# Output-projection weights loaded in runs of two rows: what follows for the head dimension, and for a kernel that waits for its loads

## The chip, the cores and the metric

The kernel runs on one core of a Trainium2 chip. The metric is the device time of one execution in microseconds (us). "Span" is the time from the first to the last instruction in the records of that execution; it is about 1.8 us shorter than the time.

## The reference, cut to what matters

```python
# B = 8 sequences, one new token each; 32 heads of 128; 4096 cached keys and values; D = 640
xn = layernorm(x)
q  = (xn @ wq)                                   # 8 x 32 heads x 128
p  = softmax(q . k_cache * 128**-0.5)            # per sequence and head, over 4096 keys
o  = p . v_cache                                 # 8 x 32 x 128
out = x + o.reshape(8, 32 * 128) @ wo + mlp(layernorm(xn))      # wo: 4096 x 640
```

Everything is bf16. The two caches are 537 MB together (64 loads of 4 MB each); `wo` is 5.2 MB. So this is a kernel that streams memory.

## The kernel before

The work is cut into 64 tiles: `t = hg * 8 + b`, head group `hg` of 4 heads (`HT = 4`), sequence `b`. For a tile, K and V are one 4 MB load each, with 32 KB contiguous per partition. Two buffers for K, two for V. The output weights of a head group (512 rows of 640) are loaded once per 8 tiles; row `a * 128 + d` of a group goes to partition `d`, slot `a`:

```python
for hg in range(NG - 1):
    ld(hg * B + 3.65, wo_sb[:, :, :],
       lambda hg=hg: A_wo[span(hg, HT * P), :].rearrange("(a p) n -> p a n", p=P), ["wo"], "wo")
wo_last = A_wo[(H - HT) * P:H * P, :].rearrange("(a p) n -> p a n", p=P)
ld(T - 0.1, wo_sb[:, 0:HT - 1, :], wo_last[:, 0:HT - 1, :], ["wo"], "wo")     # the last group: 3 + 1 heads
ld(T - 0.09, wo_sb[:, HT - 1, :], wo_last[:, HT - 1, :], ["wo3"], "wo3")
```

The value matmuls (L621 in the profile) take V as the moving operand, four 32-key blocks of 512 columns in four column groups of the array (these matmuls overlap: 16 of them in the tail last 380 ns each by their records and 1.04 us together):

```python
r = e.matmul(PV_ps[32 * ct:32 * ct + HT * 4, t % 2, :],
             P_sb[:, i, m, :, :].rearrange("p a c -> p (a c)"),
             vv[:, 4 * m:4 * m + 4, :].rearrange("p a d -> p (a d)"),      # vv: V as p, key, d
             start=(q == 0), stop=(q == wide - 1))
```

ACT copies the result to `E_sb` (L640); small matmuls pick the right rows and turn it over (`pe_ex`, L646; in the last tile also L653), so that the head dimension lies on the partitions; then, once per two tiles, DVE divides by the row sums (L665):

```python
add("dve", np_, lambda e: e.tensor_tensor(
    dst, OT_ps.rearrange("p (a g) -> p a g", a=HT),                        # dst: oTn_sb, or oL_sb in the last group
    rinv_sb[:, g % 2, :].rearrange("p (a g) -> p a g", a=HT), ALU.mult), ...)
```

The projection multiplies slot by slot (L688 in the loop, L675 at the end). The end of the program is a chain: last quarter of the last V tile lands, 32 short value matmuls (L631), ACT copy, one small matmul, the division, eight projection matmuls, the copy to `out_sb`, the store.

Of the kernel before, what the change touches and what calls it, by code (L numbers as in the profile page):

```python
# [5 lines left out]
ALU = alu_op_type.AluOpType  # L6
# [5 lines left out]
P = 128  # L12
# [3 lines left out]
class _Op:  # L16
    __slots__ = ("pos", "seq", "eng", "fn", "R", "W", "X", "sem", "idx", "clock", "waits", "sig", "ticket", "seq2")


class _Sched:  # L20
# [12 lines left out]

    def add(self, eng, pos, fn, R=(), W=(), X=(), sem=None, sig=False):
        o = _Op()
        o.pos, o.seq, o.eng, o.fn, o.R, o.W, o.X, o.sem = pos, len(self.ops), eng, fn, R, W, X, sem
        o.sig = sig
        self.ops.append(o)
# [165 lines left out]
def bass_parallel_sum__gqa_block_cached__mixer_channel_mlp__decode_kernel(  # L204
# [13 lines left out]
    B, _, D = A_x.shape  # L218
    _, H, SK, DH = A_k_cache.shape
    F = B_w1.shape[1]  # L220
    HT = 4
# [3 lines left out]
    T = NG * B  # L225
    GT = 2
# [9 lines left out]
    FR = F - FC * P  # L236
    SCALE = float(DH) ** -0.5
    NK, NV, NS = 2, 2, 4
    SR = 2
    assert DH == P and D % P == 0 and H % HT == 0 and B == 8 and NJ == 128  # L240

# [3 lines left out]
    with ExitStack() as es:  # L245
# [4 lines left out]
        KV_sb = sb("KV_sb", [P, NK + NV, NJ * P], BF)  # L250
        KT_sb = sb("KT_sb", [P, NS, BK, P], BF)
        wo_sb = sb("wo_sb", [P, HT, D], BF)
# [23 lines left out]
        Y2_sb = sb("Y2_sb", [P, ND // 2, P // 2], BF)  # L276
        S_sb = sb("S_sb", [P, SR, GT, NJ], F32)
        P_sb = sb("P_sb", [P, GT, NJ // 4, HT, 4], BF)
# [7 lines left out]
        rinv_sb = sb("rinv_sb", [P, 2, HT * GT], F32)  # L286
        oTn_sb = sb("oTn_sb", [P, HT, B], BF)
        oL_sb = sb("oL_sb", [P, HT, B], BF)
# [7 lines left out]
        C2_ps = ps("C2_ps", [P, 512], F32)  # L296
        ACC_ps = ps("ACC_ps", [P, 512], F32)
        TRF = TR_ps[:, :, :].bitcast(F32)
        M1T_ps = CH_ps[0:GT, 0:P]
        NB_ps = CH_ps[:, P:P + GT]  # L300
        OT_ps = C2_ps[:, 0:HT * GT]
# [16 lines left out]
        add = sch.add  # L318
# [4 lines left out]

        def vview(t):
            return KV_sb[:, NK + t % NV, :].rearrange("p (j d) -> p j d", d=P)

        def span(i, n):

            return slice(i * n, (i + 1) * n) if isinstance(sch.turn, int) else bass.ds((sch.turn + i) * n, n)
# [22 lines left out]
        def dve_const2(e):  # L352
# [9 lines left out]
            W=["identneg", "onesb", "sel", "oTn", "wo"] + [(s, i) for s in ("Pt", "rs") for i in range(GT)])  # L362


        def ld(pos, dst, src, W, sem, R=()):
            add("sp", pos, lambda e: e.dma_start(dst, src() if callable(src) else src), R=R, W=W, sem=sem)  # L366
# [16 lines left out]
        for t in range(T):  # L383
# [5 lines left out]
            R = (["wqfree"], ["wqfree", "w1free", "hfree"])[t] if t < NV else []  # L389
# [3 lines left out]
        ld(-95.2, w1_sb, B_w1.rearrange("(k c) f -> k c f", c=DC), ["w1"], "w1")  # L393
        ld(-95.1, w2_sb[:, 0:FC, :], B_w2[0:FC * P, :].rearrange("(k c) n -> k c n", c=FC), ["w2"], "w2")
        ld(-95.0, w2_sb[0:FR, FC, :], B_w2[FC * P:F, :], ["w2r"], "w2r")
        for hg in range(NG - 1):
            ld(hg * B + 3.65, wo_sb[:, :, :],
               lambda hg=hg: A_wo[span(hg, HT * P), :].rearrange("(a p) n -> p a n", p=P), ["wo"],
               "wo")

        wo_last = A_wo[(H - HT) * P:H * P, :].rearrange("(a p) n -> p a n", p=P)
        ld(T - 0.1, wo_sb[:, 0:HT - 1, :], wo_last[:, 0:HT - 1, :], ["wo"], "wo")
        ld(T - 0.09, wo_sb[:, HT - 1, :], wo_last[:, HT - 1, :], ["wo3"], "wo3")


        def layernorm(n, pos, src, src_res, dst, dst_res):
# [21 lines left out]
        def transposed(w, pos, src, src_res):  # L428
# [16 lines left out]
            R=["x", "b2"], W=["xb2"])  # L445
# [60 lines left out]
        def scores(t):  # L506
# [27 lines left out]
            def act_s(e):  # L534
                for a in range(HT):
                    s = slice(a * PG, (a + 1) * PG)
                    r = e.activation(S_sb[s, g % SR, i, 0:JP],  # L537
                                     S_ps[s, 0:JP * HT].rearrange("p (j a) -> p j a", a=HT)[:, :, a], ACT.Copy)
                return r
            add("act", t - 0.04, act_s, R=["S"], W=[("SP", g % SR, i)], X=["S"])  # L540

# [67 lines left out]
        def values(t):  # L609
            hg, b = t // B, t % B  # L610
            g, i = t // GT, t % GT
            vv = vview(t)
            p0 = pvpos(t)
            last = t == T - 1
            NQ = NJ // 16
            wide = NQ - 2 if last else NQ
            for q in range(NQ):
                def pe_pv(e, q=q):
                    for ct in range(4):
                        m = 4 * q + ct  # L620
                        r = e.matmul(PV_ps[32 * ct:32 * ct + HT * 4, t % 2, :],  # L621
                                     P_sb[:, i, m, :, :].rearrange("p a c -> p (a c)"),
                                     vv[:, 4 * m:4 * m + 4, :].rearrange("p a d -> p (a d)"),
                                     start=(q == 0), stop=(q == wide - 1))
                    return r

                def pe_pv_last(e, q=q):
                    for ct in range(4):
                        m = 4 * q + ct
                        for c in range(4):  # L630
                            r = e.matmul(PV_ps[32 * ct:32 * ct + HT, 1 - t % 2, 0:P], P_sb[:, i, m, :, c],  # L631
                                         vv[:, 4 * m + c, :], start=(q == wide and c == 0),
                                         stop=(q == NQ - 1 and c == 3))
                    return r
                k = t % 2 if q < wide else 1 - t % 2
                add("pe", p0 + 0.02 * q + 0.1 * (q >= wide), pe_pv if q < wide else pe_pv_last,
                    R=[("V", t % NV, q), ("Pt", i)], W=[("PV", k)], X=[("PVb", k)])

            def evac(pos, k, n):
                add("act", pos, lambda e: e.activation(E_sb[:, k, 0:n], PV_ps[:, k, 0:n], ACT.Copy),  # L640
                    R=[("PV", k)] + ["wo"] * (t % GT and not last), W=[("E", k)], X=[("PVb", k)])
            OT_i = OT_ps.rearrange("p (a g) -> p a g", a=HT)[:, :, i]

            def pe_ex(e):
                for c in range(4):
                    r = e.matmul(OT_i, E_sb[:, t % 2, c * P:(c + 1) * P], sel_bf[:, c:HT * 4:4],  # L646
                                 start=(c == 0), stop=(c == 3 and not last))
                return r
            evac(p0 + (0.13 if last else 0.22), t % 2, 4 * P)
            add("pe", p0 + (0.14 if last else 0.28), pe_ex, R=[("E", t % 2), "sel"], W=["OT"], X=["C2"])  # L650
            if last:
                evac(p0 + 0.27, 1 - t % 2, P)
                add("pe", p0 + 0.28, lambda e: e.matmul(OT_i, E_sb[:, 1 - t % 2, 0:P], sel2_bf[:, :], start=False,  # L653
                                                       stop=True), R=[("E", 1 - t % 2), "sel"], W=["OT"], X=["C2"])

        def finish(g):
            hg, b0 = g // GPH, (g % GPH) * GT
            np_ = pvpos(g * GT + GT - 1) + 0.38

            tail = g >= NGRP - GPH  # L660
            res = "oL" if tail else "oTn"
            dst = (oL_sb if tail else oTn_sb)[:, :, b0:b0 + GT]
            if g <= NGRP - GPH + 1:
                add("dve", np_ - 0.004, lambda e: e.memset(oTn_sb[:, :, :], 0.0), W=["oTn", "oTn0"])  # L664
            add("dve", np_, lambda e: e.tensor_tensor(  # L665
                dst, OT_ps.rearrange("p (a g) -> p a g", a=HT),
                rinv_sb[:, g % 2, :].rearrange("p (a g) -> p a g", a=HT), ALU.mult),
                R=["OT", ("rinv", g % 2), "oTn0"], W=[res], X=["C2"])

        w = D // 2  # L670

        def pe_last(e, heads):
            for a in heads:
                for k in range(2):
                    r = e.matmul(TRF[32 * k:32 * k + B, 0, 0:w], oL_sb[:, a, :], wo_sb[:, a, k * w:(k + 1) * w],  # L675
                                 start=False, stop=(a == HT - 1), skip_group_check=True)
            return r
        LAST = pvpos(T - 1) + 0.4
        add("pe", LAST, lambda e: pe_last(e, range(HT - 1)), R=["wo", "oL", "base_ps"], X=[("TR", 0)])
        add("pe", LAST + 0.01, lambda e: pe_last(e, [HT - 1]), R=["wo3"], W=["fin"], X=[("TR", 0)])  # L680

        def project(g):

# [16 lines left out]
        def pe_zero(e):  # L700
            for n in range(2):
# [4 lines left out]
                                          start=True, stop=False, skip_group_check=True),  # L706
            R=["zeros"], W=["ACC"], X=["ACC"])
# [14 lines left out]
        def pe_hidden(e):  # L722
# [10 lines left out]
            R=[it_h], W=["h"], X=[it_h])  # L733

        def pe_hidden_t(e):
# [7 lines left out]
            R=[it_t], W=["hT"], X=[it_t])  # L743

        def pe_mlp2(e):
# [11 lines left out]
            R=["mlp", "xb2"], W=["xb2"], X=[("PVb", 0), ("PVb", 1)])  # L757
# [6 lines left out]
            R=["ACC"], W=["resT"], X=["ACC"])  # L764
# [21 lines left out]
        for pos, n in ((pvpos(T - 2) + 0.25, 2), (pvpos(T - 1) + 0.075, 4), (pvpos(T - 1) + 0.115, 3), (pvpos(T - 1) + 0.2, 1)):  # L786
# [3 lines left out]
            R=["fin"], W=["out0"], X=[("TR", 0)])  # L790
        add("act", END + 2, lambda e: e.activation(out_sb[:, w:D], TRF[32:32 + B, 0, 0:w], ACT.Copy),
            R=["fin"], W=["out1"], X=[("TR", 0, "act")])
# [51 lines left out]
```

## Time and profile before

| | |
|---|---|
| time, median of 3 | 1290.62 us |
| span of the profiled run | 1288.9 us |
| moved by DMA | 552 MB, 428 GB/s |
| busy: DVE, PE, ACT | 87%, 50%, 39% |

From the page of the kernel before: the head line and the busy shares of its engines, three rows in 40 slices of the span (digits are tenths; PEclk is the granted clock of the tensor engine), the count of DMA packets by size, the chain of waits by engine, and the DMA queue that loads instructions.

```profile
span 1288.9 us, 19855 instructions
...
PE 644.0 (50%) x7931; PEld 408.5 (32%) x7934; DVE 1121.8 (87%) x584; ACT 497.2 (39%) x1243; POOL 0.2 (0%) x4
...
PEclk9955555555655555555555555656556555555557
DMA  9999999999999999999999999999999999999998
...
DMA packets 23536, 552.00 MB, mean 428 GB/s; under 512 B 2313, under 2 KB 6497, under 8 KB 6498
...
q8 instruction: 8, 0.13, 0.0%
...
DMA 80%; DVE 9%; PE 8%; issue 3%; ACT 0%; SPq 0%; DVEq 0%
```

The DMA row is full from end to end: the loads are the bound. DVE at 87% looks close, but it is slack: it waits for K, 74.9 us in all. Of the 6497 packets under 2 KB, 2313 are tiny and 4184 have 1280 bytes; 4096 of these are rows of `wo`.

From the timeline of the kernel before, the DMA issues of the sync engine around one weight load and at the next (columns: start, duration of the issue, queue, line, operation, destination and source):

```profile
410.32 0.38 SPq L366 DMA_DIRECT2D wo_sb<-in_A_wo_dram  x1
422.45 0.33 SPq L366 DMA_DIRECT2D KV_sb<-in_A_k_cache_dram  x1
...
441.81 0.33 SPq L366 DMA_DIRECT2D KV_sb<-in_A_k_cache_dram  x1
...
463.07 0.33 SPq L366 DMA_DIRECT2D KV_sb<-in_A_k_cache_dram  x1
...
567.55 0.38 SPq L366 DMA_DIRECT2D wo_sb<-in_A_wo_dram  x1
```

A weight load is queued at 410.32 and the next one, a head group later, at 567.55: 157.23 us for 8 tiles and one weight load. Usually K loads are issued 19.4 us apart (422.45 to 441.81; 19.43 on average); in the gap in which the weights go through the queue it is 21.3 us (441.81 to 463.07). That is the price of one weight load: 1.83 us against the average.

From the timeline of the kernel before, the end of the program (columns: start, duration, engine, line, operation, out<-in with shapes, count, and in brackets the idle time before it with its releaser):

```profile
1284.25 0.65 PE L631 MATMUL PV_ps<-KV_sb,P_sb 128*4 128x128 bf16 x32 [0.70 <-DMA KV_sb<-in_A_v_cache_dram]
1285.00 0.28 ACT L640 ACTIVATE E_sb<-PV_ps 128x128 bf16<-128x128 f32 x1 [1.99 <-PE PV_ps L631]
...
1285.33 0.18 PE L653 MATMUL C_ps<-sel_bf,E_sb 128*128 128x4 bf16 x1 [0.42 <-ACT E_sb L640]
1285.55 0.17 DVE L665 TENSOR_TENSOR oL_sb<-C_ps,rinv_sb 128x8 bf16<-128x8 f32 x1 [6.17 <-PE C_ps L653]
...
1285.77 0.71 PE L675 MATMUL TR_ps<-wo_sb,oL_sb 128*8 128x320 bf16 x8 [0.26 <-DVE oL_sb L665]
...
1286.52 0.48 DVE L789 CAST out_sb<-TR_ps 8x320 bf16<-8x320 f32 x1 [0.81 <-PE TR_ps L675]
```

Here every step waits for the one before: from the division's start (1285.55) to the projection's (1285.77) it is 0.22 us, and anything added here is added to the time.

### The profile page before, as it was taken

Reading aid. Unit: us, or ns where it says so; the run is one execution under the profiler, and the core shown is the slowest. Engines: PE = TensorE matmul, PEld = TensorE weight load, DVE = VectorE, ACT = ScalarE, POOL = GpSimd, SP = SyncE. Lnnn points to the kernel's source line nnn. Section 1 sums busy time; section 2 is a strip of 40 time slices with the busy share of each in tenths; the row PEclk is TensorE's granted clock in tenths of the full one; section 3 lists DMA queues with packets and bytes.
Section 4 is the critical chain, followed back from the end, with each engine's and each line's share of the span. In section 5 each row is a group of like instructions: output and inputs, shape, how many; then the busy total and the mean of one; then the engine's idle time right before and its main releaser. Section 6 shows DMA issues by size and latency. Waiting matters only on the chain.

```text
span 1288.9 us, 19855 instructions
## 1 busy us (share of the span) xinstructions
PE 644.0 (50%) x7931; PEld 408.5 (32%) x7934; DVE 1121.8 (87%) x584; ACT 497.2 (39%) x1243; POOL 0.2 (0%) x4
## 2 busy tenths in 40 slices
PE   2654455454454455454445444444544554455456
PEld 1433233233333233233233232232332332333332
DVE  4989999898898898898988988988889888889885
ACT  1444344334344234343243442443432443423432
POOL 0000000000000000000000000000000000000000
PEclk9955555555655555555555555656556555555557
DMA  9999999999999999999999999999999999999998
GB/s 408 424 426 427 435 427 438 427 428 434 429 433 431 429 431 432 430 433 429 428 436 428 434 427 430 432 432 432 427 431 431 434 429 429 434 429 432 431 431 358
DMA packets 23536, 552.00 MB, mean 428 GB/s; under 512 B 2313, under 2 KB 6497, under 8 KB 6498
## 3 DMA queue, kind: packets, MB, share of 16 engines
q1 hardware_dynamic: 23488, 551.80, 99.9%
q8 instruction: 8, 0.13, 0.0%
q14 instruction: 6, 0.05, 0.0%
q10 hardware_dynamic: 34, 0.02, 0.0%
HBM read 551.80 MB, written 0.01 MB: 428 GB/s over the span
## 4 chain that ended last, share of the span: by engine, by line
DMA 80%; DVE 9%; PE 8%; issue 3%; ACT 0%; SPq 0%; DVEq 0%
DMA KV_sb<-in_A_v_cache_dram 76%; PE PV_ps L621 7%; DVE Y_sb L549 5%; DMA KV_sb<-in_A_k_cache_dram 2%; DVE Y_sb L553 2%; DMA KV_sb<-in_A_wq_dram 2%; DVE S_sb L556 2%; DVE M_sb L568 0%; SPq L366 0%; PE CH_ps L570 0%; PE TR_ps L675 0%; PE PV_ps L631 0%; PE TR_ps L461 0%; DVE rinv_sb L602 0%; DVEq L178 0%
## 5 line engine op out<-in xcount | busy, mean ns | idle before, releaser
L549 DVE TENSOR_TENSOR Y_sb<-KV_sb,qbc_sb 128x6144 bf16<-128x6144 bf16 x128 | 429.1, 3353 | 89.3 <-DMA KV_sb<-in_A_k_cache_dram 74.9
L556 DVE TENSOR_REDUCE S_sb<-Y_sb 128x48 f32<-128x3072 bf16 x128 | 429.2, 3353 | 4.4
L520 ACT ACTIVATE KT_sb<-TR_ps 128x1024 bf16<-128x1024 bf16 x256 | 254.6, 1020 | 228.5 <-PE TR_ps L517 227.0
L621 PE MATMUL PV_ps<-KV_sb,P_sb 128*16 128x512 bf16 x2040 | 225.0, 620 | 139.9 <-DMA KV_sb<-in_A_v_cache_dram 139.7
L517 PE MATMUL TR_ps<-ident_bf,KV_sb 128*128 128x128 bf16 x2048 | 250.2, 310 | 73.7 <-DMA KV_sb<-in_A_k_cache_dram 73.7
L553 DVE TENSOR_TENSOR Y_sb<-Y_sb 128x3072 bf16<-128x3072 bf16 x128 | 225.0, 1758 | 4.4
L517 PEld LDWEIGHTS TR_ps<-ident_bf,KV_sb 128*128 128x128 bf16 x2048 | 202.0, 142 | 84.3 <-DMA KV_sb<-in_A_k_cache_dram 78.3
L527 PE MATMUL S_ps<-qk_sb,KT_sb 128*128 128x4 bf16 x2048 | 98.2, 170 | 136.2 <-ACT KT_sb L520 134.3
L640 ACT ACTIVATE E_sb<-PV_ps 128x512 bf16<-128x512 f32 (+1 forms) x65 | 38.5, 593 | 319.1 <-PE PV_ps L621 317.1
L621 PEld LDWEIGHTS PV_ps<-KV_sb,P_sb 128*16 128x16 bf16 x2040 | 63.3, 124 | 251.8 <-DMA KV_sb<-in_A_v_cache_dram 145.2
L527 PEld LDWEIGHTS S_ps<-qk_sb,KT_sb 128*128 128x128 bf16 x2048 | 86.4, 109 | 167.4 <-ACT KT_sb L520 167.4
L588 ACT ACTIVATE P_sb<-S_sb,NB_sb 32x128 bf16<-32x128 f32 x256 | 101.9, 398 | 3.8
L646 PE MATMUL C_ps<-sel_bf,E_sb 128*128 128x4 bf16 x256 | 17.0, 172 | 135.1 <-DVE rinv_sb L602 113.2
L582 ACT ACTIVATE NB_sb<-CH_ps 128x2 f32<-128x2 f32 (+1 forms) x33 | 5.7, 172 | 171.4 <-PE CH_ps L578 171.4
L570 PE MATMUL CH_ps<-ident_f,M_sb 128*2 128x128 f32 (+1 forms) x33 | 12.1, 366 | 116.3 <-DVE M_sb L568 116.3
L646 PEld LDWEIGHTS C_ps<-sel_bf,E_sb 128*128 128x128 bf16 x256 | 11.5, 104 | 165.0 <-DVE rinv_sb L602 112.6
L537 ACT ACTIVATE S_sb<-S_ps 32x32 f32<-32x32 f32 x256 | 48.3, 189 | 32.2 <-PE S_ps L527 29.9
L588 ACT ACTIVATION_READ_ACCUMULATOR P_sb<-S_sb,NB_sb 32x1 f32 x256 | 47.0, 184 | 0.0
L570 PEld LDWEIGHTS CH_ps<-ident_f,M_sb 128*2 128x2 f32 (+1 forms) x33 | 2.7, 80 | 119.2 <-DVE M_sb L568 119.2
L664 DVE MEMSET oTn_sb<- 128x16 uint32 x30 | 2.2, 72 | 31.1 <-PE ACC_ps L688 31.1
L572 DVE TENSOR_REDUCE M_sb<-CH_ps 2x4 f32<-2x128 f32 (+1 forms) x33 | 9.2, 279 | 15.1 <-PE CH_ps L570 15.1
L599 PEld LDWEIGHTS C_ps<-rs_sb,ones_f 128*128 128x128 f32 x64 | 14.0, 274 | 25.4 <-issue 22.0
(96 smaller groups left out, 201.9 us busy)
## 6 DMA issues: line engine op xcount, KB each, us to landing
KV_sb<-in_A_k_cache_dram SPq DMA_DIRECT2D x64, 4096.0 KB, 26.8
KV_sb<-in_A_v_cache_dram SPq DMA_DIRECT2D x63, 4096.0 KB, 35.2
KV_sb<-in_A_wq_dram SPq DMA_DIRECT2D x1, 5120.0 KB, 23.8
wo_sb<-in_A_wo_dram SPq DMA_DIRECT2D x7, 640.0 KB, 30.9
KV_sb<-in_B_w_dram SPq DMA_DIRECT2D x1, 2160.0 KB, 39.1
w_sb<-in_B_w_dram SPq DMA_DIRECT2D x1, 2080.0 KB, 44.1
KV_sb<-in_A_v_cache_dram SPq DMA_DIRECT2D x1, 2048.0 KB, 12.6
KV_sb<-in_A_v_cache_dram SPq DMA_DIRECT2D x2, 1024.0 KB, 15.2
```

The source lines that it names most:

```text
L517: r = e.transpose(TR_ps[:, it.box[0], jj * P:(jj + 1) * P], kv[:, n * BK + jj, :], ident_bf[:, :])
L520: add("act", t - 0.59 + 0.12 * n, lambda e: e.activation(KT_sb[:, m % NS, :, :].rearrange("p a b -> p (a b)"), TR_ps[:, it.box[0], :], ACT ...
L527: r = e.matmul(S_ps[:, c:c + HT], KT_sb[:, m % NS, jj, :], qk_sb[:, :, i], start=True, stop=True)
L537: r = e.activation(S_sb[s, g % SR, i, 0:JP], S_ps[s, 0:JP * HT].rearrange("p (j a) -> p j a", a=HT)[:, :, a], ACT.Copy)
L549: return e.tensor_tensor(y, kv[:, j0:j1, :], qbc_sb[:, g % 2, i, :][:, None, :].to_broadcast([P, nj, P]), ALU.mult)
L553: lambda e, y=y, y2=y2: e.tensor_tensor(y2, y[:, :, 0:P // 2], y[:, :, P // 2:P], ALU.add),
L556: lambda e, y2=y2, j0=j0, j1=j1: e.tensor_reduce(S_sb[:, g % SR, i, j0:j1], y2, AX.X, ALU.add),
L570: add("pe", c - 0.715, lambda e: e.transpose(M1T_ps[0:n, :], M1_sb[:, 0:n], ident_f[:, :]), R=["M1", "identf"], W=["M1T"], X=["CH"])
L588: r = e.activation(P_sb[s, i, :, a, :], S_sb[s, g % SR, i, :].rearrange("p (m c) -> p m c", c=4), ACT.Exp, bias=NB_sb[s, g % 2, i:i + 1], ...
L621: r = e.matmul(PV_ps[32 * ct:32 * ct + HT * 4, t % 2, :], P_sb[:, i, m, :, :].rearrange("p a c -> p (a c)"), vv[:, 4 * m:4 * m + 4, :].rea ...
L640: add("act", pos, lambda e: e.activation(E_sb[:, k, 0:n], PV_ps[:, k, 0:n], ACT.Copy), R=[("PV", k)] + ["wo"] * (t % GT and not last), W=[ ...
L646: r = e.matmul(OT_i, E_sb[:, t % 2, c * P:(c + 1) * P], sel_bf[:, c:HT * 4:4], start=(c == 0), stop=(c == 3 and not last))
```

## The change

Intent: in these traces a DMA packet carries one contiguous run (32,768 bytes for a partition of K or V, 1280 for a row of `wo`). If each partition takes two adjacent rows of `wo` (2560 bytes) and not one (1280 bytes), the same bytes need half as many packets. But then partition `x * 64 + q` holds rows `d = 2q` and `d = 2q + 1` of head `2y + x` (slots `2y` and `2y + 1`), and the attention output must lie the same way. So the value matmuls read V with the head dimension as (even elements, odd elements), a step of two elements; the result has `d = 2q + r` on partition `r * 64 + q`; and the division moves four blocks of 64 partitions to their places.

```diff
+    RW, PB = 2, P // 2
+        wov = wo_sb[:, :, :].rearrange("p (y r) n -> p y (r n)", r=RW)
+        def vcols(t):
+            return KV_sb[:, NK + t % NV, :].rearrange("p (j q r) -> p j r q", q=PB, r=RW)
+        def wo_rows(src):
+            return src.rearrange("(y p r) n -> p y (r n)", p=P, r=RW)
         for hg in range(NG - 1):
-            ld(hg * B + 3.65, wo_sb[:, :, :], lambda hg=hg: A_wo[...].rearrange("(a p) n -> p a n", p=P), ["wo"], "wo")
+            ld(hg * B + 3.65, wov, lambda hg=hg: wo_rows(A_wo[span(hg, HT * P), :]), ["wo"], "wo")
-        (last group: pieces of 3 and 1 heads)
+        (last group: pieces of 2 and 2 slots, in the new order)
...
-                                     vv[:, 4 * m:4 * m + 4, :].rearrange("p a d -> p (a d)"),
+                                     vv[:, 4 * m:4 * m + 4, :, :],          # vv = vcols(t)
...
-            add("dve", np_, lambda e: e.tensor_tensor(dst, OT_ps..., rinv_sb..., ALU.mult), ...)
+            def norm(e):
+                for x in range(RW):
+                    for r in range(RW):
+                        q = slice(r * PB, (r + 1) * PB)
+                        i = e.tensor_tensor(
+                            dst[x * PB:(x + 1) * PB, r::RW, b0:b0 + GT],
+                            OT_ps.rearrange("p (a g) -> p a g", a=HT)[q, x::RW, :],
+                            rinv_sb[q, g % 2, :].rearrange("p (a g) -> p a g", a=HT)[:, x::RW, :], ALU.mult)
+                return i
...
-        pe_last: heads 0..2, then head 3 after "wo3"
+        pe_last: slots 0..1, then slots 2..3 after "wo3"
```

More of the change, by code (lines that the diff above doesn't have):

```diff
@@ L395, in bass_parallel_sum__gqa_block_cached__mixer_channel_mlp__decode_kernel @@
         ld(-95.0, w2_sb[0:FR, FC, :], B_w2[FC * P:F, :], ["w2r"], "w2r")
+        def wo_rows(src):
+            return src.rearrange("(y p r) n -> p y (r n)", p=P, r=RW)
         for hg in range(NG - 1):
-            ld(hg * B + 3.65, wo_sb[:, :, :],
-               lambda hg=hg: A_wo[span(hg, HT * P), :].rearrange("(a p) n -> p a n", p=P), ["wo"],
+            ld(hg * B + 3.65, wov,
+               lambda hg=hg: wo_rows(A_wo[span(hg, HT * P), :]), ["wo"],
                "wo")
-        wo_last = A_wo[(H - HT) * P:H * P, :].rearrange("(a p) n -> p a n", p=P)
-        ld(T - 0.1, wo_sb[:, 0:HT - 1, :], wo_last[:, 0:HT - 1, :], ["wo"], "wo")
-        ld(T - 0.09, wo_sb[:, HT - 1, :], wo_last[:, HT - 1, :], ["wo3"], "wo3")
+        wo_last = wo_rows(A_wo[(H - HT) * P:H * P, :])
+        ld(T - 0.1, wov[:, 0:HT // RW - 1, :], wo_last[:, 0:HT // RW - 1, :], ["wo"], "wo")
+        ld(T - 0.09, wov[:, HT // RW - 1, :], wo_last[:, HT // RW - 1, :], ["wo3"], "wo3")
         def layernorm(n, pos, src, src_res, dst, dst_res):
@@ L611, in values @@
             g, i = t // GT, t % GT
-            vv = vview(t)
+            vv = vcols(t)
             p0 = pvpos(t)
@@ L631, in pe_pv_last @@
                             r = e.matmul(PV_ps[32 * ct:32 * ct + HT, 1 - t % 2, 0:P], P_sb[:, i, m, :, c],
-                                         vv[:, 4 * m + c, :], start=(q == wide and c == 0),
+                                         vv[:, 4 * m + c, :, :], start=(q == wide and c == 0),
                                          stop=(q == NQ - 1 and c == 3))
@@ L661, in finish @@
             res = "oL" if tail else "oTn"
-            dst = (oL_sb if tail else oTn_sb)[:, :, b0:b0 + GT]
+            dst = oL_sb if tail else oTn_sb
             if g <= NGRP - GPH + 1:
                 add("dve", np_ - 0.004, lambda e: e.memset(oTn_sb[:, :, :], 0.0), W=["oTn", "oTn0"])
-            add("dve", np_, lambda e: e.tensor_tensor(
-                dst, OT_ps.rearrange("p (a g) -> p a g", a=HT),
-                rinv_sb[:, g % 2, :].rearrange("p (a g) -> p a g", a=HT), ALU.mult),
-                R=["OT", ("rinv", g % 2), "oTn0"], W=[res], X=["C2"])
+            def norm(e):
[7 more added lines that the diff above has]
+                return i
+            add("dve", np_, norm, R=["OT", ("rinv", g % 2), "oTn0"], W=[res], X=["C2"])
         w = D // 2
@@ L678, in bass_parallel_sum__gqa_block_cached__mixer_channel_mlp__decode_kernel @@
         LAST = pvpos(T - 1) + 0.4
-        add("pe", LAST, lambda e: pe_last(e, range(HT - 1)), R=["wo", "oL", "base_ps"], X=[("TR", 0)])
-        add("pe", LAST + 0.01, lambda e: pe_last(e, [HT - 1]), R=["wo3"], W=["fin"], X=[("TR", 0)])
+        add("pe", LAST, lambda e: pe_last(e, range(HT - RW)), R=["wo", "oL", "base_ps"], X=[("TR", 0)])
+        add("pe", LAST + 0.01, lambda e: pe_last(e, range(HT - RW, HT)), R=["wo3"], W=["fin"], X=[("TR", 0)])
         def project(g):
```

## The prediction

> **What bounds the kernel.** The DMA queue. The page's DMA row is at 9 tenths or more in all but the last of 40 slices, 428 GB/s; one queue holds 99.9% of 16 engines' span. In the chain of waits 80% is DMA, but its pieces "V landed, 3.6 us of value matmuls, next V issued" are not the real limit: a V load takes 35.2 us from issue to landing while V loads land 19.4 us apart, so the queue always holds about 16 us of work. DVE (87%) and PE (50%) follow the loads and have idle time before the K and V data (waits view: 74.9, 73.7, 139.7 us).
>
> **What the change removes.** wo_sb is loaded with runs of 2560 bytes, not 1280. By the trace's DMA packet records, a 32768-byte packet takes 1218.7 ns, an 8192-byte one 314.7, a 1280-byte one 58.2: a line of 0.0368 ns per byte plus 11 ns per packet. An estimate for 2560 bytes is then 106 ns. Each full wo load is 32 packets per engine now, 1.86 us, and 16 of about 106 ns after, 1.69 us: 0.17 us saved. This agrees with the timeline of DMA issues: K issues are 19.43 us apart on average, but 21.26 us across a wo load, 1.83 us for it. Seven such loads lie in the saturated queue: 1.2 us less. The eighth, in the tail, saves little, because the end waits for V, not wo. [...]
>
> **What it adds.** (1) The normalisation (0.17 us, once per 2 tiles) becomes four instructions. Small DVE instructions here start some 0.1 us apart, so about 0.3 us more per pair: 10 us of DVE over the run, hidden, since K is reissued 7 us before the queue gets to it. In the tail it is on the path: oL_sb, then the last matmuls. +0.3 us.
> (2) Value matmuls read V with a 4-byte step. [...] the hidden-layer matmuls, which read three of 13 elements, take 2.79 us for 5 rounds of 512 columns at a granted clock of 1.00, 0.56 us each, where value matmuls in the tail take about 0.21. In steady state the clock is 0.50 and a round of four takes 0.43 us, so I expect little or no lengthening; even doubling (3.5 to 7 us per tile) would fit PE's idle time and the queue's slack. In the tail at clock 1.00 the last 32 matmuls (0.65 us) may grow by 0 to 0.4 us, on the path; I take 0.15.
> (3) The last wo pieces become 320+320 KB, same landing: nothing.
>
> **Sum.** 1290.62 - 1.2 + 0.3 + 0.15 = 1289.9 us; range 1289.1 to 1290.9. Faster by over 2%: 0.5%; within 2%: 97.5%; slower by over 2%: 2%.
>
> **What would show it.** 2048 fewer packets under 2 KB; K issues across a wo load about 21.1 us apart; the other spacings unchanged at 19.4; still 9 tenths DMA; normalisation 128 instructions instead of 32; value-matmul bursts at 3.4 to 3.6 us; in the tail, last V landing about 1.2 us earlier and 0.3 to 0.6 us more between it and the end.
>
> **What would make it wrong.** A strided read that costs PE four times or more (14 us per tile), so that PE or V's release paces the loop; partition-shifted DVE instructions far dearer than 0.1 us; longer packets not following the line (no gain at all); wo landing late in the tail.

Two passages are cut from the text above, where the cuts are marked. They held no term of the sum, which stays 1290.62 - 1.2 + 0.3 + 0.15 = 1289.9 us. The 0.15 for the strided read was the author's estimate, taken from between the 0 and 0.4 us that the text names; no run had shown it then.

## The result, and the profile after

| | before | after |
|---|---|---|
| time, median (range), 6 runs each | 1290.66 (1290.62 to 1290.80) | 1290.48 (1290.00 to 1290.95) |
| ratio, 95% interval | | 0.9998 (0.9986 to 1.0011) |
| the same again with 5 rounds, another occasion | 1290.96 (9 runs) | 1290.35 (5 runs), ratio 0.9994 (0.9980 to 1.0007) |
| median span on that occasion | 1289.2 | 1288.5 |

A ratio is the mean time of one kernel's runs over that of the other's of the same rounds, so it is not quite the ratio of the medians quoted. The verdict is "same", inside the predicted range (1289.1 to 1290.9) and 0.6 us above its centre in the first set of runs, 0.45 in the second. Both intervals include 1, so the times alone don't show a gain: the medians differ by 0.2 us in the first set and by 0.6 in the second. The spans differ by 0.35 us in the first set (median of six 1288.55 after; only the profiled 1288.9 before) and by 0.7 in the second. What settles it is the period of the loop, below.

From the page of the changed kernel, the lines that answer to those shown of before:

```profile
span 1288.2 us, 19951 instructions
...
PE 641.0 (50%) x7931; PEld 403.3 (31%) x7934; DVE 1141.1 (89%) x680; ACT 496.9 (39%) x1243; POOL 0.2 (0%) x4
...
PEclk9755555565555655656656556555565556655556
DMA  9999999999999999999999999999999999999998
...
DMA packets 21488, 552.00 MB, mean 429 GB/s; under 512 B 2313, under 2 KB 2401, under 8 KB 4450
```

2048 packets are gone, as foreseen: 4096 of 1280 bytes became 2048 of 2560. DVE has 96 instructions more and 19.3 us more to do, and the DMA row is as full as it was.

From the timeline of the changed kernel, the weight issues that answer to 410.32 and 567.55:

```profile
409.93 0.38 SPq L372 DMA_DIRECT2D wo_sb<-in_A_wo_dram  x1
...
567.01 0.38 SPq L372 DMA_DIRECT2D wo_sb<-in_A_wo_dram  x1
```

157.08 us per head group, 0.15 less than before. Over the last four head groups the mean is 157.09 against 157.24.

From the timeline of the changed kernel, the end of the program:

```profile
1283.11 0.67 PE L640 MATMUL PV_ps<-KV_sb,P_sb 128*4 128x128 bf16 x32 [0.67 <-DMA KV_sb<-in_A_v_cache_dram]
1283.86 0.28 ACT L649 ACTIVATE E_sb<-PV_ps 128x128 bf16<-128x128 f32 x1 [1.98 <-PE PV_ps L640]
...
1284.20 0.18 PE L662 MATMUL C_ps<-sel_bf,E_sb 128*128 128x4 bf16 x1 [0.42 <-ACT E_sb L649]
1284.41 0.68 DVE L679 TENSOR_TENSOR oL_sb<-C_ps,rinv_sb 64x4 bf16<-64x4 f32 x4 [6.54 <-PE C_ps L662]
...
1285.15 0.71 PE L691 MATMUL TR_ps<-wo_sb,oL_sb 128*8 128x320 bf16 x8 [0.77 <-DVE oL_sb L679]
...
1285.90 0.48 DVE L805 CAST out_sb<-TR_ps 8x320 bf16<-8x320 f32 x1 [0.81 <-PE TR_ps L691]
```

The last V piece is there at 1283.11 and not 1284.25: 1.14 us won by then. From the division's start to the projection's it is now 0.74 us and not 0.22: 0.52 us given back. The last 32 value matmuls, with their strided read, take 0.67 us and not 0.65. What remains is 0.6 us at the last copy, 0.7 in the span. This profiled run (1290.00 us) is the fastest of its six; in the second profile of the changed kernel (a_after, 1290.36 us) the last V piece comes later, 0.79 us before that of the kernel before:

```profile
1283.46 0.67 PE L640 MATMUL PV_ps<-KV_sb,P_sb 128*4 128x128 bf16 x32 [0.66 <-DMA KV_sb<-in_A_v_cache_dram]
```

### The profile page after: what moved, and what is told of

Its sections match the earlier page's. It is cut to its first block, busy times and chain, and to the rows that moved or that the text cites. A ratio compares the mean times of both kernels' runs of the same rounds, so it can differ in the third digit from the quotient of the medians.

```text
span 1288.2 us, 19951 instructions
## 1 busy us (share of the span) xinstructions
PE 641.0 (50%) x7931; PEld 403.3 (31%) x7934; DVE 1141.1 (89%) x680; ACT 496.9 (39%) x1243; POOL 0.2 (0%) x4
## 4 chain that ended last, share of the span: by engine, by line
DMA 77%; DVE 11%; PE 8%; issue 4%; ACT 0%; SPq 0%; DVEq 0%
DMA KV_sb<-in_A_v_cache_dram 73%; PE PV_ps L630 7%; DVE Y_sb L558 6%; DVE Y_sb L562 3%; DMA KV_sb<-in_A_k_cache_dram 2%; DVE S_sb L565 2%; DMA KV_sb<-in_A_wq_dram 2%; DVE oTn_sb L679 0%; DVE M_sb L577 0%; PE CH_ps L579 0%; SPq L372 0%; DVE rinv_sb L611 0%; PE PV_ps L640 0%; PE TR_ps L691 0%; PE TR_ps L470 0%
## 5 line engine op out<-in xcount | busy, mean ns | idle before, releaser
L630 PE MATMUL PV_ps<-KV_sb,P_sb 128*16 128x512 bf16 x2040 | 222.0, 609 | 132.0 <-DMA KV_sb<-in_A_v_cache_dram 132.0
L630 PEld LDWEIGHTS PV_ps<-KV_sb,P_sb 128*16 128x16 bf16 x2040 | 60.7, 120 | 246.3 <-DMA KV_sb<-in_A_v_cache_dram 137.2
L704 PE MATMUL ACC_ps<-oTn_sb,wo_sb 128*128 128x8 bf16 x600 | 20.8, 169 | 0.0
```

What stands on the lines that cost most here:

```text
L630: r = e.matmul(PV_ps[32 * ct:32 * ct + HT * 4, t % 2, :], P_sb[:, i, m, :, :].rearrange("p a c -> p (a c)"), vv[:, 4 * m:4 * m + 4, :, :], ...
L704: r = e.matmul(ACC_ps[:, c * B:(c + 1) * B], wo_sb[:, a, c * P:(c + 1) * P], oTn_sb[:, a, :], start=False, stop=False, skip_group_check=True)
```

## The experiments

The kernels were in three groups, each beside runs of the kernel before: the first two on one chip, the third (marked "second chip" below) on another. The theory: fewer packets make the loads shorter, all along the loop; the four-block division gives part of it back, once, in the tail; the strided read is free. Rivals: nothing real changed; or the extra DVE work costs along the whole loop.

A caution about "right result": the comparison with the reference passed every kernel below, even those whose result is wrong (weights in an order that the rest doesn't follow). In this problem it does not notice the attention part, so it says nothing about the new layout either. The placement of the changed kernel, and of the version in which the tensor engine places the last pair, was checked by following the indices: slot `2y + r` of partition `x * 64 + q` gets `d = 2q + r` of head `2y + x` in both weights and outputs.

Summary (medians; "group" is the mean time from weight issue to weight issue over the last four head groups of the profiled run):

| kernel | time, us | span, us | group, us |
|---|---|---|---|
| before, first chip (10 runs) | 1290.88 | 1289.1 | 157.24 (first profile) |
| before, second chip (9 runs) | 1290.88 | 1289.0 | |
| a_after: the change | 1290.35 | 1288.5 | 157.11 |
| b_tail_as_before: change without its tail | 1290.77 | 1289.0 | 157.09 |
| c_runs2: only loop loads, 2560-byte runs | 1289.71 | 1287.9 | 157.11 |
| d_norm4: only the division in four blocks | 1291.70 | 1289.8 | 157.27 |
| f_runs4: only loop loads, 5120-byte runs | 1289.28 | 1287.4 | 157.00 |
| g_half_rows: only loop loads, 640-byte runs | 1290.83 | 1288.9 | 157.26 |
| e_step2: only V read with step 2 | 1290.98 | 1289.0 | 157.24 |
| e_step4 (second chip; one run) | 1291.36 | 1289.6 | 157.25 |
| e_step8 (second chip) | 1299.68 | 1297.9 | 157.26 |
| j_pe_places_last | 1290.06 | 1288.3 | 157.10 |
| n_even_slots_first (second chip) | 1290.10 | 1288.3 | 157.11 |
| k_unrolled_tail (second chip) | 1291.91 | 1290.1 | 157.25 |

The group is the sharpest of these numbers. The six profiles of kernels with the weight loads as before (before, d_norm4, k_unrolled_tail and the three of e_step) have 157.24 to 157.27 us, the six with two-row loads 157.09 to 157.11, whatever else was changed. The weight packets' own records say the same: the mean start of a load's packets recurs every 157.24 to 157.27 us in the first six and every 157.10 to 157.11 in the others.

### a_after: the changed kernel again

No edit.

> The changed kernel itself, again, to get its time against the kernel before more sharply. Theory A (fewer packets save 0.17 us in each of seven weight loads, 1.2 us; the four-block normalisation gives back 0.52 us in the tail, once; the strided V read gives back 0.02): the mean is 0.5 to 0.8 us below before, about 1290.0. Rival 1 (nothing real changed; the first profiled execution was a lucky one): within 0.2 us of before. Rival 2 (the extra DVE work, 19 us over the run, delays loads as well): within 0.3 us of before, with a wider spread than before.

Measured: 1290.35 us against 1290.96, ratio 0.9994 (0.9980 to 1.0007), span 1288.5 against 1289.2. 0.6 us less, as theory A has it (its absolute 1290.0 was not reached), though the interval of the times alone would not rule out "no difference".

### c_runs2: the loads alone

```diff
-            ld(hg * B + 3.65, wo_sb[:, :, :],
-               lambda hg=hg: A_wo[span(hg, HT * P), :].rearrange("(a p) n -> p a n", p=P), ["wo"],
+            ld(hg * B + 3.65, wo_sb[:, :, :].rearrange("p (y r) n -> p y (r n)", r=2),
+               lambda hg=hg: A_wo[span(hg, HT * P), :].rearrange("(y p r) n -> p y (r n)", p=P, r=2), ["wo"],
```

> Only the seven weight loads inside the loop use two-row runs; V order, normalisation and tail as before, so the result is wrong on purpose. Theory A: 1.2 us less than before, 1289.4, weight packets of 2560 bytes at about 105 ns, weight load to weight load 157.25 us down to 157.08. Rival 1: same as before. Rival 2: 1.2 us or more below before, and clearly below the kernel with the tail as before.

Measured: 1289.71 us (1289.58 to 1289.80; ratio 0.9989, 0.9975 to 1.0002), span 1287.9, which is 1.2 us under the kernel before. This is the gain of the loop loads, with nothing given back. The instructions of the engines are the same as before; only the one DMA pattern differs. The interval of the times still reaches 1; Rival 1 falls by the spans (five of 1287.8 to 1288.0, against nine of 1288.8 to 1290.9 before) and by the timeline of c_runs2, with the weight issues 157.12 us apart and the last V piece 0.92 us earlier than before:

```profile
410.01 0.38 SPq L366 DMA_DIRECT2D wo_sb<-in_A_wo_dram  x1
...
567.13 0.38 SPq L366 DMA_DIRECT2D wo_sb<-in_A_wo_dram  x1
...
1283.33 0.65 PE L631 MATMUL PV_ps<-KV_sb,P_sb 128*4 128x128 bf16 x32 [0.71 <-DMA KV_sb<-in_A_v_cache_dram]
```

### d_norm4: the four-block division alone

```diff
-            add("dve", np_, lambda e: e.tensor_tensor(dst, OT_ps..., rinv_sb..., ALU.mult), ...)
+            def norm(e):
+                for x in range(2):
+                    for r in range(2):
+                        q = slice(r * 64, (r + 1) * 64)
+                        i = e.tensor_tensor(dst[q, x::2, :], OT_ps...[q, x::2, :], rinv_sb[q, ...][:, x::2, :], ALU.mult)
+                return i
+            add("dve", np_, norm, ...)
```

> The kernel before with its normalisation in four 64-partition blocks (same partitions in and out, right result), loads and V order as before. Theory A: 0.5 us slower than before, 1291.1, all of it in the tail between the last extraction matmul and the last projection. Rival 1: same. Rival 2: 0.8 us or more slower, with later loads in the loop. If the partition shift in the changed kernel has a cost of its own, the four blocks here take clearly less than 0.68 us.

Measured: 1291.70 us, span 1289.8, 0.7 us over the kernel before (0.5 were expected; ratio 1.0004, 0.9990 to 1.0017). In the chain of the end the four blocks take 0.15, 0.17, 0.15 and 0.18 us one after the other, and the projection starts 0.74 us after the first of them (timeline lines below), the 0.52 us of the changed kernel. They keep their partitions here and take as long as the changed kernel's, so moving 64 partitions across shows no cost. The other 0.2 us of the span are not found: the group is 0.03 us longer, which would make 0.2 in seven, but that is at the limit of what I can read, and by the mean start of the weight packets the period differs from the kernel before by less than 0.01 us. Rival 2 asked for more than 0.8 and later loads; the sum of the parts also speaks against it: -1.2 (c) + 0.7 (d) = -0.5, and the change has -0.35 to -0.7 by its spans.

```profile
1285.79 0.68 DVE L670 TENSOR_TENSOR oL_sb<-C_ps,rinv_sb 64x4 bf16<-64x4 f32 x4 [6.19 <-PE C_ps L653]
...
1286.53 0.71 PE L682 MATMUL TR_ps<-wo_sb,oL_sb 128*8 128x320 bf16 x8 [0.77 <-DVE oL_sb L670]
```

### e_step2: the strided read alone

```diff
+            return KV_sb[:, NK + t % NV, :].rearrange("p (j q r) -> p j r q", q=P // 2, r=2)
-                                     vv[:, 4 * m:4 * m + 4, :].rearrange("p a d -> p (a d)"),
+                                     vv[:, 4 * m:4 * m + 4, :, :],
```

> Only the value matmuls' read of V changed to a step of two elements, everything else as before, result wrong on purpose. If a step of two is free: same as before within 0.2 us, bursts of 32 matmuls still 3.4 to 3.6 us at the throttled clock and the last 32 still 0.65 us. If it costs: the last burst and the end grow by up to 0.4 us.

Measured: 1290.98 us, span 1289.0 (1289.1 before): no difference; the last 32 matmuls take 0.67 us.

### b_tail_as_before: the change without its tail

```diff
-        (last group's weights, V order and division of the changed kernel)
+        (those of the kernel before, for t >= T - B, from functions of their own)
+                def pe_pv_tail(e, q=q):
+                    return pe_pv(e, q)
```

> Two-row runs, strided V and four-block normalisation for the first 28 tile pairs only; the last head group (its weights, its V order, its normalisation) as before. Theory A: the 1.2 us are kept and the tail's 0.52 us come back: 1289.4 us, 0.5 us under the changed kernel. Rival 1: same as before, 1290.6. Rival 2 (loss all along the run, not in the tail): no better than the changed kernel, about 1290.0 to 1290.4.

Measured: 1290.77 us, span 1289.0. A clear miss: 1.4 us over the expectation, and no better than the kernel before. The tail did come back (0.22 us from division to projection), and the group is 157.09 us, so the loop kept its gain; but the last V piece landed at 1284.25, not at 1283.3 as in c_runs2. The loss is in the last head group, before the tail. Rival 2's words ("no better than the changed kernel") fit the number but not the reason: its profile has something else that no other kernel has, five more packets on the instruction queue (13 and not 8). The scheduler of this kernel rolls equal turns into a loop; my second function made the last turns of the tensor engine differ, so they were written out as straight code (the trace has 27 loop branches of the tensor engine and not 30, the last at 1128 us and not 1246: three turns left the loop; the four of the expectation below count one that was outside it before). The next kernel tests that.

### k_unrolled_tail: only the written-out turns

```diff
+                def pe_pv_tail(e, q=q):
+                    return pe_pv(e, q)
+                wide_fn = pe_pv_tail if t >= T - B else pe_pv
```

> The kernel before, unchanged in what it computes and moves; only the last eight tiles' value matmuls come from a second function of the same content, so that the tensor engine's last four loop turns are written out, as they were in the kernel with the tail as before. If that kernel's missing 1.1 us went to the five more instruction loads of 16 KB (13 packets on the instruction queue instead of 8), this one has them too and is 0.6 to 1.1 us slower than before, span about 1289.9. If they cost nothing (and its loss lies in the mixed V order or elsewhere): same as before, span about 1289.1.

Measured: 1291.91 us, span 1290.1, 1.1 over the kernel before (1289.0 on this chip; its nine runs have spans of 1288.8 to 1289.1, the five of this kernel 1289.9 to 1290.3; ratio of times 1.0009, 0.9995 to 1.0022). Same arithmetic, same loads; the page of k_unrolled_tail differs in this line of its DMA queues (packets, MB, share):

```profile
q8 instruction: 13, 0.21, 0.1%
```

Before it was 8 packets (shown above). An instruction packet has 16 KB; the last seven of this kernel, from 1153 us on, take 1.02 to 1.11 us each by the packet records. The mean over 16 engines would be 0.2 us for five of them (an estimate: 5 x 16 KB over 428 GB/s); the loss is 1.1 us. What makes the rest is not shown: which engine each packet ran on, the trace does not tell. The packet records show a wider spread at the end: of the packets of the last two V pieces, the middle one ends 0.57 us later than in the kernel before (1280.81 against 1280.24), but the last one 1.25 us later (1284.97 against 1283.72). In b_tail_as_before, beside c_runs2, it is 0.43 and 0.90. So about half of the loss is this wider spread; why it grew is not shown. What is shown is the price of the written-out turns, and that it is as large as the miss of b_tail_as_before; that the five instruction loads, and nothing else in these turns, cause it was not tested apart.

### f_runs4: runs of four rows, loads alone

```diff
-            rearrange("p (y r) n -> p y (r n)", r=2) ... "(y p r) n -> p y (r n)", r=2
+            rearrange("p (y r) n -> p y (r n)", r=4) ... "(y p r) n -> p y (r n)", r=4
```

> Only the seven loop weight loads changed, to runs of four rows (5120 bytes), result wrong on purpose. If a packet costs 11.4 ns plus 0.0366 ns per byte, as the 1280- and 2560-byte packets say, a load is 8 packets of 199 ns, 1.59 us: 1.9 us under before and 0.6 us under the two-row loads alone, about 1289.1 by the times of the runs so far, and 157.25 us per head group become 156.98. Rival (the gain is in something that two-row runs have already taken, such as the alignment or the count of descriptors issued): no better than the two-row loads, 1289.7.

Measured: 1289.28 us, span 1287.4 (1.7 under the kernel before, 0.5 under c_runs2), packets of 199.1 ns, group 157.00 us. As expected, within 0.2 us. The gain goes on with the length of the run and the smaller number of packets (the ratio of the times, 0.9988, has an interval of 0.9974 to 1.0001; the spans, 1287.2 to 1287.5, lie under all of before).

### g_half_rows: runs of half a row, loads alone

```diff
-            ld(hg * B + 3.65, wo_sb[:, :, :], ..., ["wo"], "wo")
+            for n, res in enumerate(("wo", "wob")):
+                cols = slice(n * D // 2, (n + 1) * D // 2)
+                ld(hg * B + 3.65 + 0.001 * n, wo_sb[:, :, cols], lambda ...: A_wo[span(hg, HT * P), cols]..., [res], res)
```

> Only the seven loop weight loads changed, each to two loads of half rows (640-byte runs), right result. By the same line 64 packets of 34.8 ns, 2.23 us instead of 1.86: 2.6 us over before, about 1293.3, and 157.25 us per head group become 157.62. Rival (small packets overlap enough that their number doesn't count): within 0.5 us of before.

Measured: 1290.83 us, span 1288.9, group 157.26 us: a miss, and what the rival expected: more packets, but no loss. The packets of 640 bytes take 32.0 ns by their records and not 34.8, and even so 64 of them make 2.05 us, 0.19 more than before, where the group shows 0.03. A part of the reason can be seen in how the records add up. Stretches of the windows view around one weight load; the last two numbers are the DMA share (1.00 would be 16 engines busy throughout) and GB/s. First the kernel before, then g_half_rows:

```profile
437.00:442.00 5.00, 2.49 (x24) 0.86 (x28) 4.96 (x3) 0.00 (x0) 0.00 (x0) 0.50 1.09 436
```

```profile
437.00:442.00 5.00, 2.46 (x24) 0.83 (x28) 4.97 (x3) 0.00 (x0) 0.00 (x0) 0.50 1.13 442
```

A share over 1 (1.09 and 1.13 here) means that records overlap: more than 16 run at once. Summed from 6 us before the first to 6 us after the last weight packet of a load, the excess over 16 engines' time is 4.68 us with 1024 packets, 2.64 with 512, 1.66 with 256 and 1.21 with 128, about 3.9 ns for each packet added. Taking that off gives an estimate of what a packet costs in time:

| packet, bytes | record, ns | less 3.9, ns | per engine and load | us | against 1280: worked out | measured in the group |
|---|---|---|---|---|---|---|
| 640 | 32.0 | 28.1 | x 64 | 1.80 | +0.05 | +0.03 |
| 1280 | 58.4 | 54.5 | x 32 | 1.74 | | |
| 2560 | 105.2 | 101.3 | x 16 | 1.62 | -0.12 | -0.12 to -0.15 |
| 5120 | 199.1 | 195.2 | x 8 | 1.56 | -0.18 | -0.24 |

So the record overstates a small packet. From 1280 bytes up a packet costs about 8 ns beside its bytes by this estimate (with 0.0366 ns per byte, from the records of 1280 and 2560 bytes: (105.2 - 58.4) / 1280); the 640-byte one is cheaper than that line (28.1 - 23.4 = 5 ns). By the mean start of the weight packets the group changes by +0.01 us with 640 bytes, -0.15 with 2560 and -0.24 with 5120, so for each packet saved it is less than 1 ns from 640 to 1280 bytes, 9 from there to 2560 and 11 from there to 5120. The correction does not explain all of that; why the shortest packets cost so little, these runs don't show.

### j_pe_places_last: the tensor engine places the last pair

```diff
+            def place(e, k, c, sel, start, stop):       # last tile pair only; also the row sums
+                for x in range(RW):
+                    for r in range(RW):
+                        i_ = e.matmul(OT_ag[x * PB:(x + 1) * PB, r::RW, i],
+                                      E_sb[:, k, c * P + r * PB:c * P + (r + 1) * PB], sel(x), start=start, stop=stop, ...)
+            def norm_last(e):
+                return e.tensor_tensor(dst[:, :, b0:b0 + GT], OT_ps..., rinv_sb..., ALU.mult)
```

> The changed kernel, with only the last tile pair altered: the extraction and row-sum matmuls of that pair write their results already placed (four 64-column matmuls for one), so its normalisation is one instruction again. If the 0.52 us of the tail is the row of four vector instructions, the last projection starts some 0.4 us sooner after the last V piece (0.52 less about 0.1 for three more small matmuls): 0.4 us under the changed kernel, about 1289.9, with no new instruction loads. If the tail does not set the end: same as the changed kernel, 1290.35.

Measured: 1290.06 us, span 1288.3 (ratio 0.9991, 0.9977 to 1.0005); four of the five runs 1289.78 to 1290.20, the profiled one 1291.01. The end in the timeline of j_pe_places_last:

```profile
1285.65 0.23 PE L671 MATMUL C_ps<-sel_bf,E_sb 128*64 128x2 bf16 x4 [0.43 <-ACT E_sb L657]
1285.93 0.17 DVE L707 TENSOR_TENSOR oL_sb<-C_ps,rinv_sb 128x8 bf16<-128x8 f32 x1 [6.66 <-PE C_ps L671]
...
1286.15 0.71 PE L717 MATMUL TR_ps<-wo_sb,oL_sb 128*8 128x320 bf16 x8 [0.27 <-DVE oL_sb L707]
```

The division is one instruction again, 0.22 us to the projection, and four small matmuls take 0.05 us longer than one. From the ACT copy's start to the last copy's it is 1.58 us (before 1.52, changed kernel 2.04). That the profiled run is the slow one seems to have another cause: its granted clock was still 0.50 until 1282, and the tensor engine, which fills waits with dummy matmuls in the tail, was late for the last V piece (its matmuls start at 1284.56 without waiting for the load). In the other profiles the clock had risen by about 1281.

### n_even_slots_first: start the projection after two blocks

```diff
+            def norm_slots(e, r):                        # blocks x = 0, 1 of slots r, r + 2
+                ...
+                for r in range(RW):
+                    add("dve", np_ + 0.001 * r, lambda e, r=r: norm_slots(e, r), ..., W=["oL%d" % r], ...)
+        add("pe", LAST, lambda e: pe_last(e, (0, 2)), R=["wo", "wo3", "oL", "oL0", "base_ps"], ...)
+        add("pe", LAST + 0.01, lambda e: pe_last(e, (1, 3)), R=["oL1"], W=["fin"], ...)
```

> The changed kernel; only in the last tile pair the four normalisation blocks are ordered so that weight slots 0 and 2 are complete after two of them, and the last projection starts with these. No instruction more. If the four blocks in a row are what the tail lost, two of them (0.33 us) now run beside the first four projection matmuls: span 0.3 us under the changed kernel, about 1288.2, time about 1290.0. If the weights' landing sets the last projection instead: no change, 1288.5 and 1290.35.

Measured: 1290.10 us, span 1288.3 (ratio 0.9995, 0.9981 to 1.0009). The end in the timeline of n_even_slots_first:

```profile
1284.55 0.70 DVE L688 TENSOR_TENSOR oL_sb<-C_ps,rinv_sb 64x4 bf16<-64x4 f32 x4 [6.16 <-PE C_ps L662]
...
1284.93 0.81 PE L705 MATMUL TR_ps<-wo_sb,oL_sb 128*8 128x320 bf16 x8 [0.42 <-DVE oL_sb L688]
```

The projection starts 0.38 us after the first block and not 0.74, beside the other two blocks, and takes 0.10 longer. 0.25 us of 0.52 come back, with no instruction added. Both j and n beat both kernels in the median, by 0.2 to 0.3 us against the change (for n from another chip, where the kernel before has the same median) and 0.8 against before; their intervals against the kernel before reach 1, so this is shown by the spans and the timeline and not by the ratio.

### e_step4 and e_step8: how far a read may be strided

```diff
-            ... .rearrange("p (j q r) -> p j r q", q=P // 2, r=2)
+            ... .rearrange("p (j q r) -> p j r q", q=P // 4, r=4)      # and 8
```

> Value matmuls read V with a step of four elements [...], result wrong on purpose. [...] bursts of 32 stay at 3.4 to 3.6 us. [...] a burst takes about 1.7 times as long, 5.9 us, still hidden by the loads.

> The same with a step of eight elements[...]. Both readings expect longer bursts: 2 times or more, 7 to 12 us for 32 matmuls. Up to about 10 us per tile the loads hide it in the loop, and only the last pieces (0.65 us for the last 32, perhaps 1.3 to 2.2) show in the time: 1 to 3 us slower than before. If the tensor engine then paces the loop: tens of us or more.

Measured: e_step4 1291.36 us in one run, e_step8 1299.68 us (ratio 1.0069, 1.0054 to 1.0084). Neither expectation for step 4 is met: a burst in the loop takes 3.80 us, in the tail twice as long as before. For step 8 the burst is as expected, but the loss of 8.8 us is far over the 1 to 3 expected. The timeline's value matmuls, a burst of 32 in the loop (mean granted clock in the 3.5 us from 656.7: 0.53, 0.50, 0.50 and 0.55 in the order below; with step 8 it is 0.79 over the whole burst) and the burst of 16 in the tail at full clock. Before, then step 2, 4 and 8:

```profile
656.83 3.43 PE L621 MATMUL PV_ps<-KV_sb,P_sb 128*16 128x512 bf16 x32 [1.28 <-DMA KV_sb<-in_A_v_cache_dram]
...
1279.27 1.04 PE L621 MATMUL PV_ps<-KV_sb,P_sb 128*16 128x512 bf16 x16
```

```profile
656.82 3.59 PE L624 MATMUL PV_ps<-KV_sb,P_sb 128*16 128x512 bf16 x32 [1.28 <-DMA KV_sb<-in_A_v_cache_dram]
...
1279.60 1.11 PE L624 MATMUL PV_ps<-KV_sb,P_sb 128*16 128x512 bf16 x16
```

```profile
656.66 3.80 PE L624 MATMUL PV_ps<-KV_sb,P_sb 128*16 128x512 bf16 x32 [1.29 <-DMA KV_sb<-in_A_v_cache_dram]
...
1279.37 2.03 PE L624 MATMUL PV_ps<-KV_sb,P_sb 128*16 128x512 bf16 x16
```

```profile
656.84 7.39 PE L624 MATMUL PV_ps<-KV_sb,P_sb 128*16 128x512 bf16 x32 [1.09 <-DMA KV_sb<-in_A_v_cache_dram]
...
1284.04 3.77 PE L624 MATMUL PV_ps<-KV_sb,P_sb 128*16 128x512 bf16 x16
```

With step 8, 16 matmuls take 3.7 us in the loop's bursts and 3.77 in the tail, although the clock differs (16 of the 32 ran in the stretch with 0.55; from 660 to 680 us, with another burst of 7.39 us, the mean is 0.67, and in the tail 1.00): at this step the read sets the pace, not the clock of the array. With step 4 the tail doubles and the loop hardly changes. Four streams of 512 columns are 3.77 / 4 = 0.94 us with step 8 and 2.03 / 4 = 0.51 with step 4. So from step 4 to step 8 the time nearly doubles with the step. If a step of two went the same way, it would need half of the 0.51, about 0.25 us (an estimate from step 4 alone), next to the 0.26 us of the contiguous read at full clock (1.04 / 4) and far below its 0.43 at half clock (3.43 / 8). This fits what is seen, though why the time goes with the step is not shown: the change's step of two costs 0.02 us in the tail's last 32 matmuls and nothing in the loop (bursts of 3.4 to 3.6 us are found with and without it), and at full clock it is the longest of the three that is nearly free. The loop hid even 7.4 us per tile: the group of e_step8 is 157.26 us. Its 9 us are all in the last head group and the tail.

## Why the prediction was right, point by point

- **The bound.** Right. The DMA row stayed full, 19 us of extra DVE work and even 4 us per tile of extra PE work (e_step8) did not lengthen the group by more than 0.03 us.
- **Fewer packets, "1.2 us less".** Right in kind and nearly in size: c_runs2, which has only this, is 1.2 us faster by its span, and in the changed kernel the last V piece is 1.14 us earlier in one profile and 0.79 in the other. K issues across a weight load are 21.10 us apart (441.42 to 462.52), 21.1 predicted. The figure under it, 0.17 us per load, was partly luck: it came from packet records, which overlap, and the same records missed g_half_rows by 0.4 us per load. The groups show 0.15, so seven loads explain about 1.05. Whether the last 0.1 to 0.2 is more than the scatter between runs is open. For one packet these runs show about 8 ns beside its bytes from 1280 bytes up, by the estimate above, where the prediction read 11 ns off the records.
- **The division in the tail, "+0.3 us".** Right place, mis-sized: 0.52 us measured. I took "some 0.1 us apart" from other instructions, at the program's start (seven starts from 6.77 to 7.30 us), most of them on SBUF. These are TENSOR_TENSORs that read PSUM, and follow each other at 0.15 to 0.18 us; which of the two makes the difference was not tested.
- **The strided read, "I take 0.15".** Right that it is nearly free, and the allowance was too large: 0.02 us in the tail, none in the loop.
- **The sum, 1289.9.** Predicted -0.75. The measured terms are -1.05 to -1.2, +0.52 and +0.02, together -0.5 to -0.7; the spans show -0.35 and -0.7 in the two sets, the times -0.2 and -0.6 (1290.48 and 1290.35). The division was taken 0.2 us too small and the read 0.13 too large, so these two nearly cancel, which is luck. The range was wide enough that "no gain" (1290.66) would have lain in it too, so it is the timeline that confirms the mechanism, and not the number.
- **"Slower by over 2%: 2%"** for a stride that might pace the loop: the runs show how far off that was. Even a step of eight costs 0.7%.

The gain is small because it could only be small: 5.2 MB of 552 go through these packets, 1.8 us per head group, and the change saves under a tenth of that.

## What to carry to other kernels

When the DMA queue is full from end to end, look at the packets that are short, count them, and take the cost of one from what the period shows, not from the packet records alone: they overlap (a DMA share of 1.13 was read here). What this layout change added to other engines was free while they waited for loads (19.3 us more of DVE, and the group did not grow), and cost in full in the tail (0.52 us), where each small DVE instruction is about 0.17 us in a row; there, let the consumer start on the part that is finished, or let the matmul write its result in place. And watch the code size: three written-out turns cost this kernel 1.1 us and came with five more instruction loads.
